# Layer 2's x of the second and third pair of chunks: transposed by DMA in two planes of half words

## The chip, the cores and the metric

The kernel runs on one core of one Trainium2 chip. The metric is the device time of an execution in microseconds; three runs of the kernel before gave 473.83, 473.84 and 474.53 us, median 473.84. Engines: PE is TensorE (PEld its weight loads), DVE is VectorE, ACT is ScalarE, POOL is GpSimd, SP is SyncE, which here issues the DMAs and passes on waits.

## The reference

A gated linear attention over 768 positions feeds two feed-forward layers on 1536 tokens (two batches of 768) of 320 features, with 1536 hidden features. The change lies in the second layer:

```python
def _moe2_ref(x, w_gate, w_val, w_out, rms_g) -> np.ndarray:
    rms = np.sqrt(np.mean(x * x, axis=-1, keepdims=True) + 1e-06)
    xn = x / rms * rms_g
    g = xn @ w_gate
    silu = g * (1.0 / (1.0 + np.exp(-g)))
    val = xn @ w_val
    return (silu * val @ w_out).astype(np.float32)
```

## The kernel before

**The last stage.** The 1536 tokens are 12 chunks of 128. Layer 2 takes them four at a time (512 columns), as three *pairs* (each holds a pair of stretches of both batches). For every pair and each of the 12 blocks f of 128 hidden features there is one *step* of the last loop; `seq` lists the 36 steps, 0 to 35, of which the loop runs 5 to 35 (the first five are in the plan ahead of it). Step 12 is the first of the second pair, step 24 the first of the third.

**A step.** Products are made in two float32r parts: a matrix has a high part, rounded by a copy, and a low part, what the rounding left, found by a subtraction. The array is used as two halves of 64 rows (`HALF`), so that two matmuls run side by side. In step i PE does, in this order: `r_up(i, 0)`, 16 matmuls of 512 columns that begin gate (bank tag g) and value (tag a) of this step from xT and the weights w; `r_out` of step i-2, its second part, 320 columns each; `r_up(i, 1)`, 14 matmuls that end gate and value; `r_out` of step i-1, its first part. Beside it, ACT makes the sigmoid of g (`w_sg`, line 670, tile p), DVE multiplies by g and by a (`w_m1`, `w_m2`, line 234), ACT copies the result to the high part (`w_h`, line 240, tile fb) and POOL subtracts for the low part (`w_hl`, line 134, tile ft). fb and ft are what `r_out` reads one and two steps later.

**The input of a pair.** xT, the transposed x of 512 tokens, has its high part in tile xT and its low part in a tile wraw. Its four chunks are transposed while the pair before is at work: entry `ev` maps step 12c - X1[i], with X1 = (5, 4, 3, 2), to chunk i of pair c, so steps 7, 8, 9, 10 and 19, 20, 21, 22 have one chunk each. In such a step ACT copies the last 64 of the 320 features twice into rem (`x_r`), PE transposes xn in six pieces of 64 rows into a bank of tag g (`r_xp`, line 663: two column blocks of xn and rem, first the upper, then the lower rows), and at the step's end ACT copies the bank to xT (`x_h`, line 240) and DVE subtracts for the low part (`x_l`, line 134). `ORD` gives the order in which `r_up` reads the parts: the high part in the first five pairs of matmuls, the low part in the last three.

**What sets the order.** Each engine's instructions run in the order in which the code writes them (`pin`). The two halves of the array may not run ahead of one another without bound: `r_group` begins a group of matmuls, and `behind` puts an instruction on SP's queue that waits for the last matmul of the group before the last; the first matmul of the new group waits for it. So SP's queue carries, besides the DMAs, one such instruction for every group. `split` says how the 12 slots of a step's `r_out` are divided between the next step and the one after; in steps whose successor has a chunk to transpose it is 9 and 3 slots in four groups, else 6 and 6 in two. The output of a pair is copied and stored two steps after its last one.

**Tiles.** p2 has two buffers of each tag. "raw" and "wc" hold weights until about step 5.

Of the kernel before, what the change touches and what calls it, by code (L numbers as in the profile page):

```python
# [7 lines left out]
F32 = mybir.dt.float32  # L8
F32R = mybir.dt.float32r
BF16 = mybir.dt.bfloat16  # L10
I32 = mybir.dt.int32
U16 = mybir.dt.uint16
# [7 lines left out]
L = 128  # L20
# [8 lines left out]
WC = 960  # L29
# [9 lines left out]
X1 = (5, 4, 3, 2)  # L39
# [58 lines left out]
def mlstm_moe_kernel(ctx, tc, gate_if, gate_s, qk, qg, tok, w1, w2, rms_g, cst, out):  # L98
    nc = tc.nc
# [4 lines left out]
    p2 = pool("p2", 2)  # L104
# [5 lines left out]
    def bank(tag):  # L110
        return (ps_2 if tag in "ag" else ps_1).tile([128, 512], F32, tag=tag, name=tag)
# [3 lines left out]
    ident = cs[:, 0:128]  # L115
# [17 lines left out]
    def sub(eng, out, a, b):  # L133
        eng.tensor_tensor(out=out, in0=a, in1=b, op=ALU.subtract)  # L134
# [43 lines left out]
    wg_t, wo_t, wraw, wc, conv, o32 = {}, {}, {}, {}, {}, {}  # L178
# [52 lines left out]
    v, g_, a_ = nc.vector, nc.gpsimd, nc.scalar  # L231
# [7 lines left out]
    def copy(out, x, scale=1.0):  # L239
        a_.activation(out=out, in_=x, func=AF.Copy, scale=scale)  # L240

    keep = {}
    part = {}
# [71 lines left out]
    xT, xps = {}, {}  # L315
# [174 lines left out]
    def x_r(key, x):  # L490

        rem = keep["rem", key] = p1.tile([128, 2, 64], F32, tag="rem", name="rem")
        copy(rem, x[:, 256:320].unsqueeze(1).to_broadcast([128, 2, 64]))

    def x_p(key, x, tag):
# [2 lines left out]
            nc.tensor.transpose(out=ps[:, 128 * k:128 * k + 128], in_=x[:, 128 * k:128 * k + 128], identity=ident)  # L498
        nc.tensor.transpose(out=ps[:, 256:384], in_=keep.pop(("rem", key)).rearrange("p b n -> p (b n)"), identity=ident)

    def x_h(key, t, i):
        copy(t()[0][:, :, i * L:(i + 1) * L], xps[key][:, 0:384].rearrange("p (s t) -> p s t", s=3))

    def x_l(key, t, i):
        n = slice(i * L, (i + 1) * L)
        sub(v, t()[1][:, :, n], xps.pop(key)[:, 0:384].rearrange("p (s t) -> p s t", s=3), t()[0][:, :, n])
# [22 lines left out]
    def new_xT2(pair, part):  # L529
        t = xT.setdefault((2, pair), [])  # L530
        if part == len(t):
            if part == 0:
                t.append(p2.tile([128, 6, T], F32R, tag="xT", name="xT").rearrange("p s t -> p (s t)"))
            else:
                t.append(p2.tile([128, WC], I64, tag="wraw", name="wraw").bitcast(F32R)[:, 0:6 * T])
            t[part] = t[part].rearrange("p (s t) -> p s t", s=3)
        return t
# [8 lines left out]
    hst, o_ps, xn, n_out, xl = {}, {}, {}, {}, {}  # L546
# [53 lines left out]
    def w_up(k, f, m):  # L600
        g = keep["w", k, f, m] = bank("ga"[m])
        x, w = xT[k], wg_t[f]
        for i, (ws, xs) in enumerate(ORD):
            nc.tensor.matmul(out=g, lhsT=w[:, m, ws, :], rhs=x[xs // 3][:, xs % 3, :], start=(i == 0), stop=(i == 7))  # L604
# [5 lines left out]
    HALF = slice(0, 64), slice(64, 128)  # L610
    groups = []

    def tie(a, b):
        tc.add_manual_dep(a, b.name, mybir.DependencyInfo(mybir.DependencyClass.Sync, mybir.DependencyReason.DATA), reason="bank")

    def behind(k, last):
        n = nc.sync.nop().ins
        tie(n, last)
        tie(k, n)
# [5 lines left out]
    def r_mm(**kw):  # L625
        k = nc.tensor.matmul(**kw).ins  # L626
        if not groups[-1] and len(groups) > 2:
            behind(k, groups[-3][-1])
        groups[-1].append(k)

    def r_up(k, f, ph):
        if ph == 0:
            keep["w", k, f, 0], keep["w", k, f, 1] = bank("g"), bank("a")
        x, w = xT[k], wg_t[f]
        r_group()
        for i, (ws, xs) in enumerate(ORD[:8 - ph]):
            for r in range(2):
                m = r ^ ph
                n = HALF[r]
                r_mm(out=keep["w", k, f, m], lhsT=w[n, m, ws, :], rhs=x[xs // 3][n, xs % 3, :], start=(ph == 0 and i == 0), stop=(ph == 1 and i == 6))  # L640
# [3 lines left out]
    def r_out(k, f, slots):  # L644
        h = hst[k, f]
        r_group()
        for s in slots:
            js = JS[s // 3]
            hs, ws = ((0, 0), (0, 1), (1, 0))[s % 3]
            for r, j in enumerate(js):  # L650
                key = k + (j,)
                if key not in o_ps:
                    o_ps[key] = bank(f"o{j}")
                n = HALF[r]
                r_mm(out=o_ps[key][:, 0:DM], lhsT=h[hs][n, j * L:(j + 1) * L], rhs=wo_t[f][n, ws, :], start=(f == 0 and s < 6 and s % 3 == 0), stop=(f == NF - 1 and s > 5 and s % 3 == 2))

    def r_xp(key, x, r):
        if r == 0:
            xps[key] = bank("g")
        ps, n = xps[key], HALF[r]  # L660
        for i in range(3):
            t = x[n, 128 * i:128 * i + 128] if i < 2 else keep["rem", key][n].rearrange("p b n -> p (b n)")
            k = nc.tensor.transpose(out=ps[:, 128 * i + 64 * r:128 * i + 64 * r + 64], in_=t, identity=ident[n, n]).ins
            if r and i == 0:
                behind(k, keep["lower"])
        keep["lower"] = k

    def w_sg(k, f):
        s = keep["ws", k, f] = p2.tile([128, 4, L], F32, tag="p", name="p").rearrange("p u t -> p (u t)")
        a_.activation(out=s, in_=keep["w", k, f, 0], func=AF.Sigmoid)  # L670

    def w_m1(k, f):
        s = keep["ws", k, f]
        tt(v, s, s, keep["w", k, f, 0], ALU.mult)

    def w_m2(k, f, n=slice(0, 512)):
        s = keep["ws", k, f]
        tt(v, s[:, n], s[:, n], keep["w", k, f, 1][:, n], ALU.mult)

    def w_h(k, f, n=slice(0, 512)):  # L680
        if (k, f) not in hst:
            hst[k, f] = [p2.tile([128, 4, L], F32, tag=tag, name=tag).bitcast(F32R).rearrange("p u t -> p (u t)") for tag in ("fb", "ft")]
        copy(hst[k, f][0][:, n], keep["ws", k, f][:, n])

    def w_hl(k, f, n=slice(0, 512), eng=None):
        h = hst[k, f]
        sub(eng or g_, h[1][:, n], keep["ws", k, f][:, n], h[0][:, n])
# [129 lines left out]
    for c in range(NC):  # L817
        for b in range(B):
# [40 lines left out]
            key = (1, c, b)  # L859
            op(f"XR{c}{b}", lambda key, c, b: x_r(key, rows(c, b)), key, c, b)  # L860
            op(f"XP{c}{b}", lambda key, c, b, tag: x_p(key, rows(c, b), tag), key, c, b, ("o0", "o1")[b] if c == 0 else "o2" if c > 2 else "a")
            i = b + 2 * (c == 5)
            op(f"XH{c}{b}", x_h, key, lambda c=c: new_xT(c), i)
            op(f"XL{c}{b}", x_l, key, lambda c=c: new_xT(c), i)
    for f in range(NF):
# [25 lines left out]
        for n, k in enumerate(((1, 4), (2, 0))):  # L891
            if n and f >= NP:
                continue
            p = "pq"[n]
# [46 lines left out]
    t = bank("o0")  # L941
# [25 lines left out]
    ev = {}  # L967
    for c in range(1, NC // 2):
        for i in range(4):
            ev[12 * c - X1[i]] = (2, 4 * c + i), lambda c=c, part=1: new_xT2(c, part), i, xn[4 * c + i]  # L970

    def last_out(k):

        for n in range(2):
            ot = p2.tile([128, 8 * 122], F32, tag="tok", name="ot")[:, 0:2 * DM].rearrange("p (b n) -> p b n", b=2)
            for b in range(2):
                o = o_ps[k + (2 * n + b,)][:, 0:DM]
                if b:
                    v.tensor_copy(out=ot[:, b], in_=o)
                else:  # L980
                    copy(ot[:, b], o)
            r0 = (2 * k[1] + n) * L
            stores.append((out.rearrange("(b s) n -> s b n", b=B)[r0:r0 + L], ot))

    def store():
        for o, i in stores:
            nc.sync.dma_start(out=o, in_=i)
        stores.clear()
# [3 lines left out]

    split = {}
    for i in range(len(seq)):
        split[i] = ((range(0, 3), range(3, 6), range(6, 9)), range(9, 12)) if i + 1 in ev else ((range(0, 6),), range(6, 12))
    split[end - 2], split[end - 1] = ((), range(0, 6)), ((), None)
    for i in range(NP, len(seq)):
        k, f = seq[i]
        x = ev.get(i)
        if i == NP:  # L1000
            for m in range(2):
                w_up(k, f, m)
        else:
            r_up(k, f, 0)
            r_out(*seq[i - 2], split[i - 2][1])
            r_up(k, f, 1)
        if i > 1 and seq[i - 2][1] == NF - 1:
            last_out(seq[i - 2][0])
        if x:
            x_r(x[0], x[3])  # L1010
        w_sg(k, f)
        w_m1(k, f)
        if x:
            new_xT2(x[0][1] // 4, 0)
            r_xp(x[0], x[3], 0)
        for n in split[i - 1][0]:
            r_out(*seq[i - 1], n)
        if x:
            r_xp(x[0], x[3], 1)
            keep.pop(("rem", x[0]))  # L1020
        store()
        cuts = [slice(0, 256), slice(256, 512)] if i == end else [slice(0, 512)]
        for n in cuts:
            w_m2(k, f, n)
            w_h(k, f, n)
        for n in cuts:
            w_hl(k, f, n, v if i == end else g_)
        if x:
            x_h(x[0], x[1], x[2])
            x_l(x[0], x[1], x[2])  # L1030
        if i == NP:
            for key in LATE.split():
                part.pop(key)()
# [90 lines left out]
```

## Time and profile before

| what | value |
| --- | --- |
| median of three runs | 473.84 us |
| the profiled execution, its own time | 475.06 us |
| its span, first to last instruction | 473.2 us |
| PE busy | 463.4 us, 98% of the span |
| DVE, ACT, POOL busy | 263.3, 203.7, 202.0 us |
| granted TensorE clock, mean | 0.989 |
| last stage (steps 5 to 35) | from about 300 us on |

The profiled execution has 1.9 us outside its span. In the profile, a row of a timeline is an instruction or several alike in a row, with its start from the span's begin and its duration; in square brackets stands how long its engine had been idle and what ended that. The starts of steps, read from PE's first `r_up` matmul after an `r_out`, are 310.51 (step 7), 338.44 (12), 375.03 (19) and 402.97 (24).

### The profile page before, as it was taken

The numbers are of one execution on the slowest core, as the hardware profiler recorded it, in microseconds if no ns is written. First come the engines' busy times: TensorE is split into PE (matmuls) and PEld (weight loads), VectorE is DVE, ScalarE is ACT, GpSimd is POOL, SyncE is SP. The second block draws the span as 40 slices with busy tenths as digits, with TensorE's granted clock in tenths as the row PEclk, the third lists the DMA queues.
The fourth block names the chain that finished last, engine by engine and source line by source line (L and its number), as shares of the span: only waits on it lengthen the run. The fifth ranks groups of instructions, "written<-read, shape, count | busy, mean of one in ns | idle before, by whom it ended". The sixth has DMA issues, their size and how long they took to land.

```text
span 473.2 us, 9869 instructions
## 1 busy us (share of the span) xinstructions
PE 463.4 (98%) x3946; PEld 420.9 (89%) x3946; DVE 263.3 (56%) x463; ACT 203.7 (43%) x461; POOL 202.0 (43%) x245
## 2 busy tenths in 40 slices
PE   8989999899999999999999999999999999999996
PEld 5778999899999999988988888888899988999995
DVE  6689678787678887754375465423232233332223
ACT  4485575536345544552665564223232232322222
POOL 3365576665645745214574546322222322223221
PEclk9789999999999999999999999999999999999999
DMA  7799874202552222363222130000010000100001
GB/s 233 258 301 346 312 220 164 63 12 67 168 169 66 74 69 81 99 247 156 84 83 84 45 124 0 1 1 1 1 57 2 1 2 1 55 3 0 1 3 57
DMA packets 13188, 43.93 MB, mean 93 GB/s; under 512 B 1526, under 2 KB 4998, under 8 KB 13142
## 3 DMA queue, kind: packets, MB, share of 16 engines
q1 hardware_dynamic: 12998, 43.15, 27.6%
q8 instruction: 31, 0.51, 0.5%
q14 instruction: 15, 0.12, 0.1%
q10 hardware_dynamic: 144, 0.14, 0.1%
HBM read 41.24 MB, written 2.05 MB: 91 GB/s over the span
## 4 chain that ended last, share of the span: by engine, by line
PE 92%; DVE 3%; DMA 2%; ACT 1%; issue 1%; POOL 0%; SPq 0%; DVEq 0%; POOLq 0%
PE g L558 15%; PE o L626 12%; PE g L626 11%; PE a L626 11%; PE o L585 8%; PE g L604 7%; PE a L604 7%; PE o L697 6%; PE o L558 3%; PE a L427 2%; PE a L335 2%; DMA fb<-fd 2%; PE o L582 1%; PE a L425 1%; DVE ft L237 1%; PE o L943 1%
## 5 line engine op out<-in xcount | busy, mean ns | idle before, releaser
L134 POOL TENSOR_TENSOR ft<-p,fb 128x512 fp32r<-128x512 f32 x47 | 61.6, 1314 | 137.7 <-ACT fb L240 137.7
L558 PE MATMUL g<-xT,w 128*128 128x256 f32 x640 | 84.9, 288 | 1.5 <-ACT xT L240 0.8
L234 DVE TENSOR_TENSOR p<-p,g 128x512 f32<-128x512 f32 x36 | 24.8, 688 | 107.6 <-ACT p L670 107.6
L558 PEld LDWEIGHTS g<-xT,w 128*128 128x128 f32 x640 | 80.9, 194 | 2.5 <-ACT xT L240 1.3
L626 PE MATMUL a<-xT,w 64*128 64x512 f32 x300 | 79.5, 392 | 0.0
L626 PE MATMUL g<-xT,w 64*128 64x512 f32 x300 | 79.5, 392 | 0.0
L670 ACT ACTIVATE p<-g 128x512 f32<-128x512 f32 x48 | 28.6, 597 | 83.1 <-PE a L626 62.1
L626 PE MATMUL o<-w,fb 64*128 64x320 f32 x512 | 60.2, 311 | 0.0
L134 POOL TENSOR_TENSOR h<-sig,h 128x256 fp32r<-128x256 f32 x42 | 36.8, 877 | 50.7 <-ACT h L240 48.3
L240 ACT ACTIVATE fb<-p 128x512 fp32r<-128x512 f32 (+1 forms) x49 | 30.2, 622 | 62.8 <-DVE p L234 52.7
L626 PEld LDWEIGHTS a<-xT,w 64*128 64x128 f32 x300 | 52.6, 184 | 3.1
L626 PEld LDWEIGHTS g<-xT,w 64*128 64x128 f32 x300 | 52.7, 184 | 3.0
L626 PEld LDWEIGHTS o<-w,fb 64*128 64x128 f32 x512 | 48.4, 185 | 3.7 <-issue 0.4
L585 PE MATMUL o<-w,h 128*128 128x320 f32 x252 | 47.0, 318 | 0.0
L234 DVE TENSOR_TENSOR p<-p,a 128x512 f32<-128x512 f32 (+1 forms) x49 | 33.1, 676 | 20.6 <-PE a L604 12.9
L626 PE MATMUL a<-wraw,w 64*128 64x512 f32 x150 | 44.1, 390 | 0.0
L626 PE MATMUL g<-wraw,w 64*128 64x512 f32 x150 | 44.1, 390 | 0.0
L626 PE MATMUL o<-w,ft 64*128 64x320 f32 x256 | 43.1, 305 | 0.0
L585 PEld LDWEIGHTS o<-w,h 128*128 128x128 f32 x252 | 37.8, 189 | 1.1
L134 POOL TENSOR_TENSOR w<-wc,w 128x256 fp32r<-128x256 f32 (+2 forms) x37 | 27.5, 752 | 19.5 <-ACT w L240 15.0
L626 PEld LDWEIGHTS g<-wraw,w 64*128 64x128 f32 x150 | 27.6, 184 | 2.5
L626 PEld LDWEIGHTS a<-wraw,w 64*128 64x128 f32 x150 | 27.7, 184 | 2.4
(176 smaller groups left out, 904.0 us busy)
## 6 DMA issues: line engine op xcount, KB each, us to landing
wraw<-in_w_dram SPq DMA_DIRECT2D x24, 959.8 KB
tok<-in_tok_dram SPq DMA_DIRECT2D x10, 488.0 KB
fb<-fd SPq DMA_DIRECT2D x18, 256.0 KB
raw<-in_qk_dram SPq DMA_DIRECT2D x24, 160.0 KB
out_dram<-ot SPq DMA_DIRECT2D x6, 320.0 KB
qg<-in_qg_dram SPq DMA_DIRECT2D x8, 180.0 KB
early<-in_tok_dram SPq DMA_DIRECT2D x2, 488.0 KB
early<-fd SPq DMA_DIRECT2D x2, 256.0 KB
```

Of the source, the lines that this page charges most:

```text
L134: eng.tensor_tensor(out=out, in0=a, in1=b, op=ALU.subtract)
L234: eng.tensor_tensor(out=out, in0=a, in1=b, op=op)
L237: v.tensor_tensor_scan(out=out, data0=a, data1=b, initial=initial, op0=op0, op1=op1)
L240: a_.activation(out=out, in_=x, func=AF.Copy, scale=scale)
L335: nc.tensor.matmul(out=st[j][:, i * L:(i + 1) * L], lhsT=t[n, 1, i, :], rhs=t[n, 0, i, :], start=True, stop=True)
L427: nc.tensor.matmul(out=ps[:, (o + i) * E:(o + i + 1) * E], lhsT=p[:, i, :], rhs=w[:, o + i, :], start=True, stop=True)
L558: nc.tensor.matmul(out=g[:, m, :], lhsT=w[:, m, ws, :], rhs=x[xs // 3][:, xs % 3, :], start=(i == 0), stop=(i == 7))
L585: nc.tensor.matmul(out=o, lhsT=h[:, hs, b * L:(b + 1) * L], rhs=wo_t[f][:, ws, :], start=(n == 1 and i == 0), stop=(n == NF and i == 2))
L604: nc.tensor.matmul(out=g, lhsT=w[:, m, ws, :], rhs=x[xs // 3][:, xs % 3, :], start=(i == 0), stop=(i == 7))
L626: k = nc.tensor.matmul(**kw).ins
L670: a_.activation(out=s, in_=keep["w", k, f, 0], func=AF.Sigmoid)
L697: nc.tensor.matmul(out=o_ps[key][:, 0:DM], lhsT=h[hs][:, n], rhs=wo_t[f][:, ws, :], start=(c == 1 and i == 0), stop=(c == NF and i == 2))
```

## The change

The chunk of x goes another way. POOL copies xn, seen as 16-bit words, into two planes (`d_planes`): the low halves of the 384 columns and the high halves, where the last 64 columns stand twice. One DMA on SP's queue transposes both planes at once, six blocks of 128x128 half words from one part of the tile to the other (`d_move`; in the built program a DMA_TRANSPOSE of 48 tiles of 16x128). POOL puts the halves together again (`d_join`), and `x_h` and `x_l` read the joined tile in SBUF. The four actions lie in three steps: planes in step 12c - X1[i] - 1, the DMA in the next, join, `x_h` and `x_l` in the one after; for the second pair planes in 6 to 9, DMAs in 7 to 10, joins and `x_h` in 8 to 11. The transposes by PE, rem and its copy are gone, and every step's `r_out` is divided 6 and 6.

```diff
@@ -498,6 +498,25 @@
             nc.tensor.transpose(out=ps[:, 128 * k:128 * k + 128], in_=x[:, 128 * k:128 * k + 128], identity=ident)
         nc.tensor.transpose(out=ps[:, 256:384], in_=keep.pop(("rem", key)).rearrange("p b n -> p (b n)"), identity=ident)
 
+    def d_planes(key, x):
+        t = xps[key] = p2.tile([128, 8 * L], F32, tag="raw", name="xw").bitcast(U16)
+        w, h = t[:, 0:6 * L].rearrange("p (two n) -> p two n", two=2), x.bitcast(U16).rearrange("p (n two) -> p two n", two=2)
+        g_.tensor_copy(out=w[:, :, 0:320], in_=h)
+        g_.tensor_copy(out=w[:, :, 320:384], in_=h[:, :, 256:320])
+    def d_move(key):
+        t = xps[key]
+        nc.sync.dma_start_transpose(out=t[:, 6 * L:12 * L].rearrange("p (s t) -> p s t", t=L), in_=t[:, 0:6 * L])
+    def d_join(key):
+        t = xps[key]
+        x = p2.tile([128, WC], I32, tag="wc", name="xw")[:, 0:3 * L]
+        g_.tensor_copy(out=x.bitcast(U16).rearrange("p (n two) -> p two n", two=2), in_=t[:, 6 * L:12 * L].rearrange("p (two n) -> p two n", two=2))
+        xps[key] = x.bitcast(F32)
     def x_h(key, t, i):
         copy(t()[0][:, :, i * L:(i + 1) * L], xps[key][:, 0:384].rearrange("p (s t) -> p s t", s=3))
 
@@ -653,17 +672,6 @@
                     o_ps[key] = bank(f"o{j}")
                 n = HALF[r]
                 r_mm(out=o_ps[key][:, 0:DM], lhsT=h[hs][n, j * L:(j + 1) * L], rhs=wo_t[f][n, ws, :], start=(f == 0 and s < 6 and s % 3 == 0), stop=(f == NF - 1 and s > 5 and s % 3 == 2))
-
-    def r_xp(key, x, r):
-        if r == 0:
-            xps[key] = bank("g")
-        ps, n = xps[key], HALF[r]
-        for i in range(3):
-            t = x[n, 128 * i:128 * i + 128] if i < 2 else keep["rem", key][n].rearrange("p b n -> p (b n)")
-            k = nc.tensor.transpose(out=ps[:, 128 * i + 64 * r:128 * i + 64 * r + 64], in_=t, identity=ident[n, n]).ins
-            if r and i == 0:
-                behind(k, keep["lower"])
-        keep["lower"] = k
 
     def w_sg(k, f):
         s = keep["ws", k, f] = p2.tile([128, 4, L], F32, tag="p", name="p").rearrange("p u t -> p (u t)")
@@ -967,7 +975,9 @@
     ev = {}
     for c in range(1, NC // 2):
         for i in range(4):
-            ev[12 * c - X1[i]] = (2, 4 * c + i), lambda c=c, part=1: new_xT2(c, part), i, xn[4 * c + i]
+            e = (2, 4 * c + i), lambda c=c, part=1: new_xT2(c, part), i, xn[4 * c + i]
+            for n in range(3):
+                ev[n, 12 * c - X1[i] + n - 1] = e
 
     def last_out(k):
 
@@ -992,11 +1002,11 @@
 
     split = {}
     for i in range(len(seq)):
-        split[i] = ((range(0, 3), range(3, 6), range(6, 9)), range(9, 12)) if i + 1 in ev else ((range(0, 6),), range(6, 12))
+        split[i] = (range(0, 6),), range(6, 12)
     split[end - 2], split[end - 1] = ((), range(0, 6)), ((), None)
     for i in range(NP, len(seq)):
         k, f = seq[i]
-        x = ev.get(i)
+        x = [ev.get((n, i)) for n in range(3)]
         if i == NP:
             for m in range(2):
                 w_up(k, f, m)
@@ -1006,18 +1016,16 @@
             r_up(k, f, 1)
         if i > 1 and seq[i - 2][1] == NF - 1:
             last_out(seq[i - 2][0])
-        if x:
-            x_r(x[0], x[3])
         w_sg(k, f)
         w_m1(k, f)
-        if x:
-            new_xT2(x[0][1] // 4, 0)
-            r_xp(x[0], x[3], 0)
         for n in split[i - 1][0]:
             r_out(*seq[i - 1], n)
-        if x:
-            r_xp(x[0], x[3], 1)
-            keep.pop(("rem", x[0]))
+        if x[1]:
+            d_move(x[1][0])
+        if x[2]:
+            d_join(x[2][0])
+        if x[0]:
+            d_planes(x[0][0], x[0][3])
         store()
         cuts = [slice(0, 256), slice(256, 512)] if i == end else [slice(0, 512)]
         for n in cuts:
@@ -1025,9 +1033,10 @@
             w_h(k, f, n)
         for n in cuts:
             w_hl(k, f, n, v if i == end else g_)
-        if x:
-            x_h(x[0], x[1], x[2])
-            x_l(x[0], x[1], x[2])
+        if x[2]:
+            new_xT2(x[2][0][1] // 4, 0)
+            x_h(*x[2][:3])
+            x_l(*x[2][:3])
         if i == NP:
             for key in LATE.split():
                 part.pop(key)()
```

**PE at the start of step 12.** In the built order (line 626 before is 645 in the changed kernel; o0 to o3 are the banks of the output) PE stands before at the end of step 11 and the begin of step 12 as follows:

```order
L626 MATMUL o2_3687<-w_3630,ft_4228 128x320
L626 MATMUL o3_3703<-w_3630,ft_4228 128x320
L626 MATMUL g_4295<-xT_3949,w_3146 128x512 [waits SP_sequencer_49,DVE_49]
L626 MATMUL a_4296<-xT_3949,w_3146 128x512
L626 MATMUL g_4295<-xT_3949,w_3146 128x512
...
L626 MATMUL g_4295<-wraw_3984,w_3146 128x512
```

and in the changed kernel:

```order
L645 MATMUL o2_3687<-w_3630,ft_4194 128x320
L645 MATMUL o3_3703<-w_3630,ft_4194 128x320
L645 MATMUL g_4271<-xT_4046,w_3146 128x512 [waits SP_sequencer_49,DVE_49,Activation_49]
L645 MATMUL a_4272<-xT_4046,w_3146 128x512 [waits DVE_49]
L645 MATMUL g_4271<-xT_4046,w_3146 128x512
...
L645 MATMUL g_4271<-wraw_4047,w_3146 128x512 [waits DVE_49]
```

The first matmul of the step now waits for ACT as well, and the first that reads the low part (tile wraw) for DVE.

**ACT in steps 10 to 12.** Before, from the rem copy of step 10's chunk on, to the sigmoid of step 12 (line 670):

```order
L240 ACTIVATE rem_4192<-xn_3037 128x128 [waits Activation_49]
L670 ACTIVATE p_4194<-g_4151 128x512 [waits PE_49,Pool_49]
L240 ACTIVATE fb_4227<-p_4194 128x512 [waits DVE_49]
L240 ACTIVATE xT_3949<-g_4197 128x3x128 [waits PE_49]
L670 ACTIVATE p_4274<-g_4233 128x512 [waits PE_49,Pool_49]
L240 ACTIVATE fb_4291<-p_4274 128x512 [waits DVE_49]
L670 ACTIVATE p_4342<-g_4295 128x512 [waits PE_49,Pool_49]
```

and in the changed kernel, from the sigmoid of step 10 (line 678) to that of step 12:

```order
L678 ACTIVATE p_4173<-g_4126 128x512 [waits PE_49,Activation_49]
L240 ACTIVATE fb_4193<-p_4173 128x512 [waits DVE_49]
L240 ACTIVATE xT_4046<-xw_4190 128x3x128 [waits Pool_49]
L678 ACTIVATE p_4246<-g_4199 128x512 [waits PE_49,Activation_49]
L240 ACTIVATE fb_4265<-p_4246 128x512 [waits DVE_49]
L240 ACTIVATE xT_4046<-xw_4262 128x3x128 [waits Pool_49]
L678 ACTIVATE p_4318<-g_4271 128x512 [waits PE_49,Activation_49]
```

Before, the last xT copy of the pair stands between the fb copy of step 10 and the sigmoid of step 11, now between the fb copy of step 11 and the sigmoid of step 12; and there is one in step 10 as before, which is that of the third chunk.

On POOL's queue, where each step had one subtraction (ft), there are now up to three copies ahead of it: the join, which waits for a DMA's landing, and the two copies of the planes. On SP's queue the four DMA_TRANSPOSE of a pair stand between the instructions of `behind`, each after the one for its step's last group of `r_out` and ahead of the one for the next step's first `r_up`.

## Rows read from the trace of the kernel before

**Rows 1.** Parts 1 and 4 of the page: busy time, and shares of the chain by engine
```profile
PE 463.4 (98%) x3946; PEld 420.9 (89%) x3946; DVE 263.3 (56%) x463; ACT 203.7 (43%) x461; POOL 202.0 (43%) x245
...
PE 92%; DVE 3%; DMA 2%; ACT 1%; issue 1%; POOL 0%; SPq 0%; DVEq 0%; POOLq 0%
```

**Rows 2.** Windows: stretch, its length, busy us (instructions) of each engine, PEclk, DMA
```profile
core 0: us, PE busy (x) PEld busy (x) DVE busy (x) ACT busy (x) POOL busy (x), PEclk, DMA share, GB/s
310.51:338.44 27.93, 27.93 (x298) 24.66 (x296) 9.11 (x14) 8.45 (x19) 6.49 (x5) 1.00 0.01 1
338.44:375.03 36.59, 36.59 (x383) 33.48 (x381) 10.56 (x16) 9.48 (x17) 9.08 (x7) 1.00 0.06 19
375.03:402.97 27.94, 27.94 (x298) 24.83 (x296) 9.11 (x14) 8.45 (x19) 6.50 (x5) 1.00 0.01 2
```

**Rows 3.** Instructions of line 663: duration ns min/median/max, first and last start
```profile
L663 PE MATMUL g<-cs,xn x32: 213/218/223, 314.9 to 398.0; 64*128 64x64 f32 x32
```

**Rows 4.** Timeline of PE in step 12: start us, us, instruction
```profile
338.44 0.38 PE L626 MATMUL a<-xT,w 64*128 64x512 f32 x1
...
341.17 0.38 PE L626 MATMUL g<-xT,w 64*128 64x512 f32 x1
...
343.08 0.32 PE L626 MATMUL o<-w,ft 64*128 64x320 f32 x2
```

**Rows 5.** Timelines of ACT in steps 10, 11 and 23, and of POOL
```profile
334.31 0.63 ACT L240 ACTIVATE fb<-p 128x512 fp32r<-128x512 f32 x1 [1.55 <-DVE p L234]
334.85 0.47 ACT L240 ACTIVATE xT<-g 128x384 fp32r<-128x384 f32 x1
337.86 0.60 ACT L670 ACTIVATE p<-g 128x512 f32<-128x512 f32 x1 [2.54 <-PE a L626]
340.01 0.63 ACT L240 ACTIVATE fb<-p 128x512 fp32r<-128x512 f32 x1 [1.55 <-DVE p L234]
...
404.54 0.63 ACT L240 ACTIVATE fb<-p 128x512 fp32r<-128x512 f32 x1 [1.55 <-DVE p L234]
...
340.78 1.30 POOL L134 TENSOR_TENSOR ft<-p,fb 128x512 fp32r<-128x512 f32 x1 [4.40 <-ACT fb L240]
```

**Rows 6.** Timelines of ACT and PE early in the kernel, where PE waits
```profile
27.22 0.87 ACT L240 ACTIVATE xT<-o 128x384 fp32r<-128x384 f32 x2
...
28.14 0.85 PE L558 MATMUL g<-xT,w 128*128 128x256 f32 x5 [0.78 <-ACT xT L240]
29.68 0.85 PE L558 MATMUL g<-xT,w 128*128 128x256 f32 x4 [0.69 <-DVE xT L134]
```

**Rows 7.** Windows with the granted clock (PEclk), columns as in rows 2
```profile
30.14:33.55 3.41, 3.41 (x19) 3.41 (x18) 3.31 (x3) 3.09 (x8) 2.52 (x4) 0.50 1.10 266
88.17:91.58 3.41, 3.41 (x29) 3.41 (x28) 3.41 (x3) 0.81 (x2) 2.16 (x4) 1.00 0.00 0
91.58:95.00 3.42, 1.97 (x17) 1.84 (x16) 3.39 (x7) 1.85 (x6) 1.79 (x2) 1.00 0.39 124
```

**Rows 8.** Groups of POOL's instructions by line and form: busy us, mean ns, idle before
```profile
L134 POOL TENSOR_TENSOR ft<-p,fb 128x512 fp32r<-128x512 f32 x47 | 61.6, 1314 | 137.7 <-ACT fb L240 137.7
...
L247 POOL COPY ident<-cs 128x512 f32<-128x512 f32 x1 | 0.6, 611 | 0.8 <-DMA cs<-in_cst_dram 0.8
```

**Rows 9.** SP's DMA issues by line (as rows 3), and SP's waits (total, times, longest us)
```profile
L141 SPq DMA_DIRECT2D raw<-in_qk_dram x24: 281/322/448, 2.1 to 175.8; - x24
...
L184 SPq DMA_DIRECT2D wraw<-in_w_dram x24: 327/340/572, 7.9 to 276.6; - x24
...
L987 SPq DMA_DIRECT2D out_dram<-ot x6: 372/398/408, 346.8 to 469.4; - x6
...
SPq L184 <- DMA wraw<-in_w_dram: 23.4, 7, 4.6
...
SPq L262 <- DMA fm<-gates: 2.4, 1, 2.4
```

## The prediction

> **What bounds the kernel now.** I read the page first: its busy times and its chain of work that ended last. TensorE (PE) is busy for 98% of the span and carries 92% of the chain [rows 1], so only what changes PE's own row of work, or makes PE stop, moves the time. The stage that the change touches is the last one (layer 2, from about 300 us on). There I counted time by steps; a step is one pass of the loop, and begins with its first up matmul. The sums over windows of each engine's busy time show that PE is busy for the whole of every window from step to step, at a granted clock of 1.00 [rows 2]: the steps are limited by PE alone. Seven steps without a transpose take 36.59 us, 5.23 each. The five steps 7 to 11, which transpose the four chunks of the second pair, take 27.93 us, and the five steps 19 to 23 take 27.94 us [rows 2].
>
> **What is taken from PE.** Each chunk has six 64-row transposes, each pair four chunks; 32 of the 48 read xn [rows 3], the other 16 read rem. Their durations overlap their neighbours', so I don't sum them, I take the steps: 27.93 - 5 x 5.23 = 1.80 us, and 1.81 us for the second pair. This contains the transposes, the later start of the matmuls behind them and the other division of the out matmuls, all of which the change takes away, since steps 7 to 11 become like the seven clean ones. Gain: 3.6 us. The ScalarE copy into rem goes as well; ScalarE waits for others in this stage, so it counts for nothing.
>
> **What is put on the path: two waits at the chunk boundaries.** This term decides. Before, the last chunk of a pair was transposed in step 10 (22), so a whole step lay between its x_h and x_l and the first up matmul of step 12 (24), which reads all four chunks of xT. Now the fourth chunk has its planes in step 9, its DMA in step 10 and its join and x_h in step 11, and the first up matmul of step 12 has a wait on ScalarE that it didn't have. ScalarE works in order, and x_h stands behind the fb copy of step 11. When is that? PE begins step 12 at 338.44 [rows 4]. ScalarE's fb copy of step 11 starts at 340.01 [rows 5], since it needs both halves of step 11's up results, the sigmoid and two VectorE products. In step 10, where x_h also stands behind fb, it starts 0.54 us after fb does (334.31 and 334.85) and takes 0.47 us. So x_h of step 11 ends at 340.01 + 0.54 + 0.47 = 341.02. The only row where PE visibly waits for an xT copy shows 0.05 us from its end (27.22 + 0.87) to PE's start at 28.14 [rows 6]. PE would start step 12 at 341.07 instead of 338.44: 2.63 us idle. The same sum at the second boundary, from 404.54 and the step's start at 402.97 (where the last window of rows 2 ends): 404.54 + 1.01 + 0.05 - 402.97 = 2.63. Both: 5.3 us. All of it is lost, since PE has no slack in any step to win it back. The copy now reads SBUF, not PSUM; fb, an SBUF copy of 512 columns, takes 0.63, so 0.63 is the upper bound for x_h, which makes 5.6 for both. x_l is not late: the low half is read at the sixth pair of matmuls, some 1.1 us into the step, and x_l ends about 0.6 us after x_h.
>
> **The clock.** A stop of 2.6 us in dense work has no precedent in this trace. [...] I take 1.45 each, 2.9 for two. The lower bound is none (the clock holds), the upper 3.4.
>
> **What must hide behind other work.** *GpSimd's copies.* Each chunk adds 640 + 128 + 768 half words per partition. The bounds are GpSimd's two rows of 512 elements: a plain copy 611 ns, a two-input subtraction 1314 ns [rows 8], so 1.8 to 3.9 us per chunk, 3.1 to 5.2 with the subtraction that each step has anyway. I take the plain copy, the same kind of operation. GpSimd is idle for 4.40 of a step's 5.23 us by waiting [rows 5], and its result, done at 340.78 + 1.30 = 342.08, is first used by PE at 343.08 [rows 4]: a full microsecond more. Nothing of it shows, up to the upper bound. *The landing.* The chunk's transpose can go out when PE ends the out matmuls in the middle of a step, 2.50 us before the next step (in step 12: 341.17 against a next start at 338.44 + 5.23). Its join must be over when fb of the step after is done; that leaves 2.50 - 0.4 + 5.23 + 2.11 - 2.0 = 7.4 us for the transfer (0.4 for the issue, below; 2.11 from a step's start to the place of x_h, 340.55 - 338.44; 2.0 for the join, the upper price). No transpose by DMA is in the trace. DMAs whose landing someone waited for: 2.4 us (40 KB), at the longest 4.6 us (960 KB) [rows 9]; this one moves 192 KB. I take 3 us: hidden.
> [...]
> *SP's queue.* PE's groups of matmuls are chained through SP: the first matmul of each waits for an SP instruction that waits for the group before the last. The transpose is queued between two of these; if SP is held by it for over 2.50 us (less two semaphore hops), the next step's first matmul waits for SP, eight times. SP's issues take 0.32, 0.34 and 0.40 us for 160, 960 and 320 KB [rows 9], so size doesn't lengthen them, and I take 0.4: hidden. The upper bound is one such issue for each of the 48 tiles of 16x128 that the instruction names, 15 us.
>
> **The sum.** -3.6 + 5.3 + 2.9 = +4.6 us. The rows come from an execution of 475.06 us (span 473.2, 1.9 around it), 1.2 above the median of 473.84; that offset lies in no term, so I add to the median: 478.4 us.
>
> **Rivals.** (1) *The waits come, the clock holds.* Same stops, no fall: -3.6 + 5.3 = 1.7, 475.5. [...] A fall at only one boundary would give 477.0 and belongs to the forecast's range. (2) *SP is held by the transpose.* Decides from 2.5 us on; each microsecond above costs 8 us; held 4 us: 478.4 + 12 = 490. Against: the issues of three sizes take much the same. For: none of them is a transpose, and a cost for each of its 48 tiles need only be 52 ns to come to 2.5 us. (3) *Late landing.* Beyond 7.4 us each microsecond holds ScalarE and delays x_h at both boundaries, 2 us in all; at 10 us, 483.6. (4) *Not slower.* If the stop at a boundary were under 1.8 us, the change would pay. It would need x_h of step 11 to end before 340.24, at the time at which fb itself has just begun; only a chain shorter by 0.8 us from step 11's sigmoid on would do that, for instance if removing the PSUM reads of the transposes sped up ScalarE and VectorE in these steps. At 1.3 us per boundary without a fall: 472.8. Nothing in the rows of step 11, which already has no transposes before, points to it. (5) *The change doesn't take the work off PE*: excluded, PE has 48 matmuls fewer in the built order.
>
> **Chances.** Forecast with one or two falls 0.60; (1) 0.17; (2) 0.08; (3) 0.08; (4) and whatever else would bring it level or better 0.07. A measurement of this kernel can tell some 0.2% (0.95 us) from no change. Faster 0.03, same 0.06 (the best of (4), the lower edge of (1)), slower 0.91. The range: 474.9 takes in (1) with its stops 0.3 us shorter each; upwards, 5.6 for the stops and 3.4 for the clock give 479.2, and most of (3) reaches 483.5. Outside lie (2), (4) and the end of (3), under 2 in 10.
>
> **What would show it.** Right: steps 7 to 11 at 5.23 us each; no PE gap but one of about 2.6 us before step 12 and before step 24, ended by ScalarE's xT copy; granted clock 0.50 for some 3.4 us behind each; SP's transposes under 2 us; GpSimd's two copies and its join together near 1.9 us. Wrong: PE waiting for SP in the middle of the stage; the join waiting for the DMA beyond fb; a boundary without a gap, or a gap below 1.8 us.

## The result, and the profile after

The changed kernel takes 478.81 us (median of 20 runs), the kernel before 474.23 us in runs on the same chip: a ratio of 1.009, 95% interval 1.0064 to 1.0115. The change costs 4.6 us. The profiled execution of the changed kernel took 479.06 us, its span is 477.3 us, 4.1 more than that of before. Executions of the kernel before differ by some 3 us with their mean granted clock (of 35 beside the experiments, 16 at 0.997 or more have a median of 471.4 us, the other 19 of 474.5); in the profiled execution of before, at 0.989, the clock stands at 0.50 from 16.5 to 23.3 and from 30.1 to 33.6 us [rows 7], long before the changed stage, so that windows of the last stage are free of this, medians not quite.

The page's busy times and the chain by engine say almost what they said before [rows 1]:

```profile
PE 461.9 (97%) x3896; PEld 414.9 (87%) x3898; DVE 268.7 (56%) x463; ACT 202.2 (42%) x453; POOL 219.3 (46%) x269
...
PE 92%; DVE 2%; ACT 2%; DMA 2%; issue 1%; POOL 0%; SPq 0%; DVEq 0%; ACTq 0%; POOLq 0%
```

PE is busy for 1.5 us less, and the span is 4.1 us longer: PE stands still more. Where, the windows show, cut at the starts of steps (columns as in rows 2): steps 7 to 11, the stop before step 12, step 12, steps 13 to 18, steps 19 to 23, the stop before step 24, step 24.

```profile
310.72:336.85 26.13, 26.13 (x274) 22.81 (x270) 10.89 (x13) 7.39 (x14) 14.26 (x15) 1.00 0.14 31
336.85:339.50 2.65, 0.17 (x4) 0.00 (x1) 1.40 (x3) 1.05 (x3) 0.32 (x1) 1.00 0.00 0
339.50:346.54 7.04, 7.04 (x55) 5.87 (x56) 1.37 (x1) 0.59 (x1) 0.96 (x1) 0.76 0.01 2
346.54:377.89 31.35, 31.35 (x328) 27.49 (x326) 9.17 (x14) 8.25 (x15) 8.64 (x8) 1.00 0.06 22
377.89:404.02 26.13, 26.13 (x274) 22.81 (x270) 10.90 (x13) 7.39 (x14) 14.26 (x15) 1.00 0.14 31
404.02:406.67 2.65, 0.17 (x4) 0.00 (x1) 1.39 (x3) 1.05 (x3) 0.32 (x1) 1.00 0.00 0
406.67:412.29 5.62, 5.61 (x54) 4.60 (x56) 1.38 (x1) 0.59 (x1) 0.96 (x1) 1.00 0.02 3
...
340.68:344.09 3.41, 3.41 (x24) 2.88 (x22) 0.19 (x1) 0.00 (x0) 0.00 (x0) 0.50 0.00 0
```

The five steps that contain a pair's four transposes took 27.93 and 27.94 us [rows 2]; five steps now take 26.13, 5.23 a step, as clean steps do: 3.6 us are gained. At each boundary 2.65 us pass in which PE works for 0.17. Steps 12 and 24 are longer than 5.23: 5.62 at the full clock, and 7.04 where the granted clock falls (mean 0.76; in the last window below it is 0.50 for 3.41 us). The account: -1.80 - 1.81 + 2 x 2.65 + (7.04 - 5.23) + (5.62 - 5.23) = +3.9 of the span's 4.1.

PE's and PEld's timelines at the two boundaries name who ends the stops:

```profile
339.50 0.50 PE L645 MATMUL g<-xT,w 64*128 64x512 f32 x1 [2.48 <-ACT xT L240]
...
340.93 0.28 PEld L645 LDWEIGHTS g<-wraw,w 64*128 64x128 f32 x1 [0.43 <-DVE wraw L134]
...
406.67 0.50 PE L645 MATMUL g<-xT,w 64*128 64x512 f32 x1 [2.48 <-ACT xT L240]
```

The first up matmul waits for ACT's copy into xT, 2.48 us each time. And then, 1.4 us into the step, the first weight load that goes with the low part (wraw) comes after another 0.43 us of idle PEld, ended by DVE's x_l. Step 24 is 0.39 us too long. Not all of that is x_l: step 12 of copy first below, where x_l is in time, takes 5.34 us behind its stop of 0.29, 0.11 more than a clean step; so about 0.28 us is left for x_l, an estimate from these steps. The timelines of ACT, DVE and POOL ahead of step 12:

```profile
338.40 0.63 ACT L240 ACTIVATE fb<-p 128x512 fp32r<-128x512 f32 x1 [1.55 <-DVE p L234]
338.94 0.51 ACT L240 ACTIVATE xT<-xw 128x384 fp32r<-128x384 f32 x1
...
339.48 1.40 DVE L134 TENSOR_TENSOR wraw<-xw,xT 128x384 fp32r<-128x384 f32 x1 [1.11 <-ACT xT L240]
...
339.18 1.28 POOL L134 TENSOR_TENSOR ft<-p,fb 128x512 fp32r<-128x512 f32 x1 [2.67 <-ACT fb L240]
```

x_h stands behind fb, as it did in step 10 before [rows 5]: fb starts 1.55 us after the step should have begun, x_h 0.54 later, and takes 0.51. x_l, behind it, takes 1.40 us, the first 0.98 of them beside POOL's subtraction, which ends at 340.46. In the kernel before it lay beside that subtraction too and took 0.56; POOL's and DVE's timelines in step 10 of before, and the group of x_l there (busy us, mean ns, idle before):

```profile
335.08 1.30 POOL L134 TENSOR_TENSOR ft<-p,fb 128x512 fp32r<-128x512 f32 x1 [4.37 <-ACT fb L240]
...
335.36 0.56 DVE L134 TENSOR_TENSOR wraw<-g,xT 128x384 fp32r<-128x384 f32 x1 [1.08 <-ACT xT L240]
...
L134 DVE TENSOR_TENSOR wraw<-g,xT 128x384 fp32r<-128x384 f32 x8 | 4.5, 558 | 8.6 <-ACT xT L240 8.6
```

The group of x_l in the changed kernel, and the new work on POOL (groups) and SP (duration ns min/median/max, first and last start):

```profile
L134 DVE TENSOR_TENSOR wraw<-xw,xT 128x384 fp32r<-128x384 f32 x8 | 10.8, 1354 | 8.9 <-ACT xT L240 8.9
...
L517 POOL COPY xw<-xw 128x768 uint16<-128x768 uint16 x8 | 10.4, 1304 | 0.0
L507 POOL COPY xw<-xn 128x640 uint16<-128x640 uint16 x8 | 5.8, 719 | 0.3
L508 POOL COPY xw<-xn 128x128 uint16<-128x128 uint16 x8 | 2.3, 294 | 0.0
...
L512 SPq DMA_TRANSPOSE xw<-xw x8: 1212/1214/1321, 313.7 to 396.6; - x8
```

Three copies of 0.72 + 0.29 + 1.30 = 2.3 us per chunk on POOL, and SP held for 1.21 us by each transpose. Steps 7 to 11 together are no longer for it than five clean steps.

### The profile page after: what moved, and what is told of

It reads as the page before. It is cut to its first block, busy times and chain, and to the rows that moved or that the text cites. A ratio compares the mean times of both kernels' runs of the same rounds, so it can differ in the third digit from the quotient of the medians.

```text
span 477.3 us, 9779 instructions
## 1 busy us (share of the span) xinstructions
PE 461.9 (97%) x3896; PEld 414.9 (87%) x3898; DVE 268.7 (56%) x463; ACT 202.2 (42%) x453; POOL 219.3 (46%) x269
## 4 chain that ended last, share of the span: by engine, by line
PE 92%; DVE 2%; ACT 2%; DMA 2%; issue 1%; POOL 0%; SPq 0%; DVEq 0%; ACTq 0%; POOLq 0%
PE g L577 15%; PE g L645 12%; PE o L645 12%; PE a L645 10%; PE o L604 8%; PE g L623 7%; PE a L623 7%; PE o L705 6%; PE o L577 3%; PE a L335 2%; PE a L427 2%; DMA fb<-fd 2%; PE o L601 1%; PE a L425 1%; PE o L951 1%; PE o L433 1%
## 5 line engine op out<-in xcount | busy, mean ns | idle before, releaser
L645 PE MATMUL o<-w,fb 64*128 64x320 f32 x512 | 58.4, 310 | 0.0
L645 PEld LDWEIGHTS o<-w,fb 64*128 64x128 f32 x512 | 45.9, 187 | 5.6 <-issue 0.4
L645 PE MATMUL g<-wraw,w 64*128 64x512 f32 x150 | 45.1, 397 | 0.0
L645 PE MATMUL a<-wraw,w 64*128 64x512 f32 x150 | 45.1, 397 | 0.0
L645 PE MATMUL o<-w,ft 64*128 64x320 f32 x256 | 39.8, 307 | 0.0
```

## The experiments

| kernel | median us | ratio to before | 95% interval |
| --- | --- | --- | --- |
| the change | 478.81 | 1.009 | 1.0064 to 1.0115 |
| one step earlier | 470.25 | 0.9942 | 0.9908 to 0.9976 |
| copy first | 471.62 | 0.9968 | 0.9939 to 0.9996 |
| stop filled | 476.37 | 1.007 | 1.0039 to 1.0102 |
| before, even split | 475.84 | 1.0061 | 1.003 to 1.0092 |
| each transpose twice | 485.53 | 1.0249 | 1.0206 to 1.0292 |
| first pair early only | 475.16 | 1.0025 | 0.9994 to 1.0056 |

The kernel before had medians of 473.83 us beside the first four of the experiments and 473.86 beside the last two.

**One step earlier.** The whole route is kept and moved by one step.

```diff
-X1 = (5, 4, 3, 2)
+X1 = (6, 5, 4, 3)
```

> The planes, the transposes by DMA and the join stand one step earlier, so that the last x_h and x_l of a pair of chunks are made in step 10 and step 22, not in step 11 and step 23. Theory (the two stops of 2.48 us at the starts of steps 12 and 24 are the price of where the last x_h stands, and the transposes by DMA cost nothing in themselves): no wait of TensorE over 0.3 us at either boundary, no low-clock stretch there, steps 12 and 24 about 1.4 to 1.8 us longer than a plain step or less; time 3.6 us below the kernel before, so about 470.6 (ratio 0.992). Rival (the DMA route itself, GpSimd's copies or SP's hold are what costs): 474 or more, with waits of TensorE of over 0.5 us in steps 6 to 11, where none was, behind ACT's x_h or behind SP.

Measured: 470.25 us, 3.6 below the kernel before. Windows (columns as in rows 2) of steps 8 to 12, of step 12 alone, of steps 20 to 24 and of step 24 alone:

```profile
315.56:341.69 26.13, 26.13 (x274) 23.91 (x272) 12.31 (x14) 7.80 (x14) 11.76 (x12) 1.00 0.07 16
336.46:341.69 5.23, 5.23 (x58) 4.79 (x56) 1.37 (x2) 1.23 (x3) 1.29 (x1) 1.00 0.00 0
378.28:404.41 26.13, 26.13 (x274) 23.91 (x272) 12.31 (x14) 7.81 (x14) 11.81 (x12) 1.00 0.07 17
399.18:404.41 5.23, 5.23 (x58) 4.79 (x56) 1.38 (x2) 1.23 (x3) 1.29 (x1) 1.00 0.01 3
```

Each window of five steps holds a boundary. PE is busy throughout, the first steps of the pairs take 5.23 like any other, and the clock stays at 1.00. The transposes by DMA, POOL's copies and SP's holds are all there and cost nothing: what costs is that the last x_h and x_l fall into the last step before they are needed. This kernel is faster than both.

**Copy first.** The steps stay, x_h and x_l move ahead of m2, fb and ft within the step.

```diff
+        if x[2]:
+            new_xT2(x[2][0][1] // 4, 0)
+            x_h(*x[2][:3])
+            x_l(*x[2][:3])
         for n in cuts:
             w_m2(k, f, n)
             w_h(k, f, n)
...
-        if x[2]:
-            new_xT2(x[2][0][1] // 4, 0)
-            x_h(*x[2][:3])
-            x_l(*x[2][:3])
```

> In the step, ACT makes x_h before the next step's copy of h, and VectorE makes x_l before m2; the transposes stay in their steps. Theory (the stop is the place of x_h in ACT's queue, behind the copy of h that waits for GpSimd): the stops at the starts of steps 12 and 24 shrink from 2.48 us to about 0.6, the clock does not fall there; 471.4 to 472.1 us. For x_l, which took 1.34 us beside GpSimd's subtraction: if it is the two engines at once that stretches it, about 0.56 us here; if it is that both its inputs now lie in SBUF, 1.34 again. Rival (the copy waits for the landing of the transpose or for the join, not for its place): the stops stay above 2 us, time about 478.8.

Measured: 471.62 us. Timelines at step 12 (ACT, PE, POOL, DVE), the groups of x_l and of POOL's join, and the window of step 12:

```profile
336.23 0.51 ACT L240 ACTIVATE xT<-xw 128x384 fp32r<-128x384 f32 x1
...
336.79 0.50 PE L645 MATMUL g<-xT,w 64*128 64x512 f32 x1 [0.29 <-ACT xT L240]
...
334.88 1.06 POOL L517 COPY xw<-xw 128x768 uint16<-128x768 uint16 x1
...
338.93 1.29 POOL L134 TENSOR_TENSOR ft<-p,fb 128x512 fp32r<-128x512 f32 x1 [2.99 <-ACT fb L240]
...
336.97 0.55 DVE L134 TENSOR_TENSOR wraw<-xw,xT 128x384 fp32r<-128x384 f32 x1
...
L134 DVE TENSOR_TENSOR wraw<-xw,xT 128x384 fp32r<-128x384 f32 x8 | 4.4, 551 | 0.0
...
L517 POOL COPY xw<-xw 128x768 uint16<-128x768 uint16 x8 | 8.5, 1062 | 0.0
...
336.79:342.13 5.34, 5.34 (x54) 4.68 (x56) 1.33 (x3) 1.22 (x2) 1.29 (x1) 1.00 0.01 3
```

The stop shrinks from 2.48 to 0.29 us, step 12 takes 5.34 instead of 7.04, and the clock stays at 1.00: the place of x_h in ACT's queue made the stop. (What fb waits for, by ACT's timeline further up, is DVE's product, not GpSimd as the expectation has it.) Two things are read from x_l: its operands are the same as in the change, both in SBUF, and it takes 0.55 us, since POOL is idle beside it (its copy ends at 335.94, its subtraction starts at 338.93). So the 1.35 us are the two engines at once, not the SBUF inputs alone. POOL pays as well: its join takes 1.38 us in the change where it begins while x_l still runs (1.06 in each pair's first, 1.30 on the mean), and 1.06 here.

**Stop filled.** Ten pairs of matmuls at the start of steps 12 and 24, whose results are overwritten.

```diff
+        if ph == 0 and f == 0 and k[1]:
+            for i in range(10):
+                for r in range(2):
+                    n = HALF[r]
+                    r_mm(out=keep["w", k, f, r], lhsT=wg_t[NF - 1][n, r, 0, :], rhs=xT[2, k[1] - 1][0][n, 0, :], start=True, stop=True)
```

> Twenty matmuls of 512 columns are added at the start of steps 12 and 24, into banks that the first up matmuls overwrite, so they change no value; TensorE works through most of the stop and the first up matmul still waits for x_h. Theory (of the 4.6 us a part is the clock that falls after the stop): TensorE's idle stretch at each boundary is under 0.5 us, the granted clock stays 1.00 there, the stop itself still costs its 2.5 us; time about 476.5, against 478.8 for the change. Rival (the falls have nothing to do with the stop, or all of the loss is the stop): time stays at 478 to 479, or a low-clock stretch shows at the same places.

Measured: 476.37 us. Steps 12 and 24 in windows, and the first matmul that needs xT in PE's timeline:

```profile
337.24:345.50 8.26, 8.08 (x79) 6.41 (x76) 2.77 (x3) 1.64 (x4) 1.28 (x1) 1.00 0.01 2
...
402.99:411.23 8.24, 8.05 (x78) 6.29 (x76) 2.76 (x3) 1.64 (x4) 1.27 (x1) 1.00 0.01 2
...
339.89 0.50 PE L645 MATMUL g<-xT,w 64*128 64x512 f32 x1 [0.18 <-ACT xT L240]
...
405.64 0.50 PE L645 MATMUL g<-xT,w 64*128 64x512 f32 x1 [0.19 <-ACT xT L240]
```

Each boundary costs 8.26 - 5.23 = 3.03 us, what the second one of the change costs at full clock (2.65 + 5.62 - 5.23 = 3.04). PE works instead of standing still, and the clock holds at both. Against its own runs of before this kernel is 2.5 us slower, the change 4.6; the difference of 2.0 us is put down to the clock: it is what the idle PE cost beyond the wait itself. The two intervals overlap, and both medians carry the early clock, so the 2.0 is a rough size; that there is such a price rests on the low-clock stretches in the traces.

**Before, even split.** The transposes stay on PE, layer 2's out matmuls are divided 6 and 6.

```diff
-        split[i] = ((range(0, 3), range(3, 6), range(6, 9)), range(9, 12)) if i + 1 in ev else ((range(0, 6),), range(6, 12))
+        split[i] = (range(0, 6),), range(6, 12)
```

> The kernel before with its 96 products of the layer-1 output spread six to each step, as the change spreads them; the transposes stay on TensorE. It divides the gain of TensorE (3.6 us by the sum) between the transposes that are gone and the new spread. Theory (the spread moves work only, the gain is the transposes'): within 0.3 us of the kernel before. Rival (the spread is part of the gain): 0.5 to 2 us faster. Should a step with transposes and six products become too long for its cover, up to 1 us slower.

Measured: 475.84 us, by the medians 2.0 slower than before; neither theory had it, only the last case of the expectation had the direction, with up to 1 us. Windows of steps 7 to 11, of the seven clean steps and of steps 19 to 23, and PE's first matmul behind a chunk's transposes:

```profile
306.63:336.29 29.66, 28.34 (x299) 25.26 (x297) 9.10 (x14) 8.46 (x19) 6.45 (x5) 1.00 0.01 1
336.29:372.87 36.58, 36.58 (x382) 34.87 (x380) 10.55 (x16) 9.48 (x17) 9.05 (x7) 1.00 0.06 19
372.87:402.57 29.70, 28.36 (x299) 25.27 (x297) 9.10 (x14) 8.47 (x19) 6.46 (x5) 1.00 0.01 1
...
312.63 0.49 PE L626 MATMUL g<-xT,w 64*128 64x512 f32 x1 [0.33 <-DVE p L234]
```

With transposes on PE the even split costs 29.66 - 27.93 = 1.73 us in the second pair and 29.70 - 27.94 = 1.76 in the third [rows 2], 3.5 us in all: with fewer out matmuls in the steps that transpose, the next step's first matmul is reached before DVE has done its part, and PE stands still 0.33 us in each of the four steps. The medians show only 2.0 of it, because the early clock enters them unequally: 8 of the 12 executions here have a mean granted clock of 0.997 or more, 16 of the 35 of before. The kept trace is one of the 8. Its clock in two early stretches, and that of before in the first of them (the second is in rows 7, at 0.50):

```profile
17.07:23.89 6.82, 6.21 (x47) 4.09 (x46) 5.26 (x14) 6.23 (x18) 1.88 (x4) 1.00 0.82 287
30.14:33.55 3.41, 2.65 (x23) 2.42 (x22) 3.26 (x7) 1.46 (x4) 3.02 (x6) 1.00 1.02 371
...
17.07:23.89 6.82, 6.82 (x32) 5.39 (x32) 3.60 (x12) 4.02 (x11) 0.57 (x2) 0.54 0.57 180
```

It reaches step 7 at 306.63, the kernel before at 310.51. The median of the 8 is 475.0 us, that of the 16 is 471.4, a difference of 3.6. So the split by itself gains nothing, and it is free only once the transposes are gone. The change without it (transposes gone, 9 and 3 kept) was not run, so how the 3.6 us of gain divide further is not shown.

**Each transpose twice.** On top of the early placement.

```diff
-        nc.sync.dma_start_transpose(out=t[:, 6 * L:12 * L].rearrange("p (s t) -> p s t", t=L), in_=t[:, 0:6 * L])
+        for _ in range(2):
+            nc.sync.dma_start_transpose(out=t[:, 6 * L:12 * L].rearrange("p (s t) -> p s t", t=L), in_=t[:, 0:6 * L])
```

> The placement one step earlier, with each transpose by DMA issued twice into the same place, one behind the other; the second adds no value. One issue held SP for 1.21 us. Theory (the hold is hidden as long as it is under about 2.5 us, and what SP issues behind it, the weights' DMAs above all, comes into play beyond that): SP is held for 1.21 + 1.21 us and, as the second waits for the landing of the first, for some 2 us more, so about 4.5 us; TensorE then waits up to 2 us in each of eight steps, time up to 16 us above the early placement (470.3 to 486). Rival (the bound of 2.5 us was too low, other work covers SP, since the weights are asked for more than a step ahead): no wait of TensorE of over 0.5 us in steps 5 to 11, time within 0.5 us of the early placement, about 470.3.

Measured: 485.53 us, 15.3 above the early placement. SP's timeline (the two issues and the wait between them are one row), PE's beside it, the window of that step, and a row of SP's waits (total us, times, longest):

```profile
313.03 3.71 SPq L513 DMA_TRANSPOSE xw<-xw  x2
...
316.94 0.47 PE L646 MATMUL g<-xT,w 64*128 64x512 f32 x1 [1.58 <-SPq L637]
...
309.85:316.94 7.09, 5.50 (x54) 5.20 (x55) 1.37 (x2) 1.19 (x3) 3.25 (x4) 1.00 0.25 56
...
SPq L513 <- DMA xw<-xw: 10.0, 8, 1.3
```

SP has the pair in hand for 3.71 us: two issues of 1.21 and 1.29 of waiting for the first transpose to land. PE then stands still for 1.58 us until the SP instruction that chains its groups (line 637, `behind`), and the step takes 7.09 instead of 5.23. Eight such steps are 8 x 1.86 = 14.9 us. So SP may be held for some 3.71 - 1.86 = 1.9 us before PE feels it, an estimate from this one length of hold; a single transpose, at 1.21, stays 0.6 below that. The landing is measured on the way: 1.21 + 1.29 = 2.5 us from the start of the issue.

**First pair early only.** The second pair of chunks has the early placement, the third that of the change.

```diff
-                ev[n, 12 * c - X1[i] + n - 1] = e
+                ev[n, 12 * c - X1[i] - (c == 1) + n - 1] = e
```

> The second pair of chunks has the early placement, the third pair that of the change, so that only the start of step 24 has its x_h late. Theory (each boundary has its own price, and the two add): step 12 starts with no stop; one stop of 2.48 us and a late low part of 0.4 at step 24, 3.0 us in all, and the low clock behind it in some runs (0 to 1.4 us); with the early placement at 470.25, 473.3 to 474.7. Rival (what stops at step 24 is late because of what happened at step 12): no stop at either, about 470.3.

Measured: 475.16 us, 0.5 above the upper end expected. Windows of step 12, the stop before step 24, and step 24:

```profile
336.12:341.34 5.22, 5.22 (x58) 4.78 (x56) 1.38 (x2) 1.22 (x2) 1.28 (x1) 1.00 0.00 0
...
398.83:401.48 2.65, 0.18 (x5) 0.00 (x1) 1.40 (x3) 1.05 (x3) 0.32 (x1) 1.00 0.00 0
401.48:408.65 7.17, 7.15 (x55) 5.99 (x56) 1.38 (x1) 0.59 (x1) 0.96 (x1) 0.76 0.01 2
```

The boundary with early x_h has no price, the other the whole: the second stop does not come of the first. This time the clock falls behind the stop before step 24, where in the profiled execution of the change it held: 2.65 + 7.17 - 5.22 = 4.6 us for one boundary. By the medians it is 475.16 - 470.25 = 4.9.

## Why the prediction was right

Predicted 478.4 us, measured 478.81, slower as said. The steps in turn:

- **What PE gains.** Forecast 3.6 us from the windows; steps 7 to 11 and 19 to 23 went to 26.13 us each, and the early placement, which has the gain and no stops, is 3.6 us below before. Right; the even split by itself brings none of it.
- **The stops.** Forecast 2.63 us each, measured 2.65 between the steps (2.48 of them idle): fb's start 1.55 us into the step that would have begun, x_h 0.54 behind it, as read. The small rest lies in x_h itself, 0.51 us instead of 0.47. Copy first and one step earlier show the mechanism: change the place of x_h, and the stop goes.
- **"x_l is not late."** This step failed. The prediction let x_l end 0.6 us after x_h, with its old 0.56 us. It took 1.40, because with both inputs in SBUF it is held up by POOL's subtraction, beside which it had lain before without loss. That is about 0.28 us at each boundary; 0.11 more goes at the start after a stop, as in copy first. Together 2 x 0.39 = 0.8 us that no term held. The stops with it are 2 x 3.04 = 6.1 us, not 5.3.
- **The clock.** Forecast a fall at each boundary, 1.45 us each. The 1.45 was the author's estimate, and no run shows that term; what the runs showed in its place, where the clock fell, is close to it: 7.04 - 5.62 = 1.42 us in the change, 7.17 - 5.62 = 1.55 in the last experiment. But the profiled execution of the change shows one fall, not two, and the comparison with the filled stop gives roughly 2.0 us in all instead of 2.9. Of the three stops of 2.47 to 2.48 us in the two traces, two were followed by a fall. What decides, when the stop is the same, these runs do not settle. One of the change's 20 executions has a mean granted clock of 1.00, so neither boundary fell: 474.06 us, 2.7 above the median of the 16 executions of before at 0.997 or more (471.4), where the terms without the clock give -3.6 + 6.1 = 2.5.
- **The sum.** -3.6 + 6.1 + 2.0 = 4.5, against the forecast's -3.6 + 5.3 + 2.9 = 4.6. The two errors, 0.8 up and 0.9 down, cancelled; that was luck, and the number is better than its parts. The 2.0 is itself what two medians leave over, so that this sum closes proves little; the 2.5 against 2.7 does not use it.
- **Hidden work.** POOL's copies took 2.3 us per chunk (forecast 1.8, bounds 1.8 to 3.9), SP's hold 1.21 us (forecast 0.4), the landing 2.5 (forecast 3). All stayed hidden, as the early placement shows. SP's was the closest: three times the forecast, and the cover about 1.9 us, not 2.5.
- **The rivals.** Rival 2 (SP held) is real as a mechanism and starts at about 1.9 us, but the transpose holds SP for 1.21. Rival 3 (late landing) falls with the 2.5 us for one transfer of six blocks. Rival 1 (the clock holds) is what happened at one boundary of the profiled execution. Rival 4 asked for a stop under 1.8 us; there is none in the change, and the version with a stop of 0.29 us is indeed faster than before.

## What to carry to other kernels

When work moves off the engine that bounds a kernel, ask first where the operation that now feeds its consumer stands in the queue of its own engine: here the same change is 4.6 us slower or 3.6 faster by one step of placement. For an operation whose operands change their memory, look up what runs beside it on VectorE and GpSimd; here its old duration didn't carry over (0.56 us before, 1.35 in the change). A queue that also passes on waits, as SP's does here, has a cover that can be measured by holding it twice as long, before anything else is put on it.

## What the runs showed of the hardware

- VectorE and GpSimd at once: x_l with both inputs in SBUF took 1.34 to 1.40 us beside GpSimd's subtraction and 0.55 away from it; with one input in PSUM it took 0.56 beside the same subtraction. Ahead of step 12 it began 0.30 us after GpSimd did and ended 0.42 after GpSimd's end. Had it stood still until GpSimd's end and then taken its 0.55 us, it would have come to 0.98 + 0.55 = 1.53 us, by estimate; it took 1.40.
- A transpose by DMA of 48 tiles of 16x128 half words (192 KB) holds the issuing queue for 1.21 us, three to four times an ordinary issue (0.32 to 0.40 us) [rows 9], and lands within 2.5 us of the start of its issue.
- After a stop of 2.48 us in otherwise dense work TensorE's granted clock went to 0.50 in two cases of three, at a price of 1.4 to 1.6 us; with matmuls in the stop (0.18 and 0.19 us of it idle), or with a stop of 0.29 us, it stayed at 1.00.
